# The float64 weight conversion of an attention and FFN kernel: the sign word made on GpSimd, the exponent offset in ScalarE's absolute value

## The chip, the cores and the metric

The kernel runs on one core of a Trainium2 chip. The metric is the device time of one execution in microseconds. The engines are named as in the profile: PE is TensorE's matmul and PEld its weight load, DVE is VectorE, ACT is ScalarE, POOL is GpSimd, SP the queue that issues the DMAs. Each engine takes its instructions in order; a wait on another engine is a semaphore.

## The reference

```
q, k, v: (8, 8, 576, 64) float32; tau = 0.02
scores = (q @ k^T) / 8
thresh = max(scores, -1) - tau
scores = where(scores >= thresh, scores, -1e9)
attn   = exp(scores - max(scores));  attn /= sum(attn) + 1e-9
x      = (attn @ v) as (4608, 512)
h      = maximum(x @ w_in, 0)          # w_in (512, 2048), float64
out    = (h * h) @ w_out               # w_out (2048, 512), float64
```

The two weight matrices are the only float64 inputs: a random float32-like array times a Python float stays double. No engine computes in float64, so the kernel makes float32 out of pairs of 32-bit words: the high word holds sign, 11 bits of exponent and 20 of the fraction, the low word the rest of the fraction.

## The kernel before, in words

The program has two large parts. In the first (some 500 us) the attention runs in **periods** `p`; in each, two units of 128 query rows by two heads go through a software pipeline: scores on PE, four row maxima ("top", line 452) on DVE, exponentials ("pow", 462) on ACT, four threshold masks with sums ("mask", 467) on DVE, transposes of the weights (fills U, V, W; line 380) on PE with evictions on ACT (523), and the product with v (532) on PE. Small steps in between: "leastA" and "leastB" (459) add tau to the maxima and "over" (474) adds 1e-9 to the sums of the period before, all on GpSimd; "inv" (477) is the reciprocal of what "over" made, on DVE. The second part computes the FFN with a fast matrix multiplication in seven products at two levels; the weights' sums are made on GpSimd in the periods behind the conversion.

The order of every engine's work in a period is written out by hand as a list of step names: `PLAIN` for ordinary periods and `CONVERTING` (597) for periods 2 to 34, in which weights are converted. A name of this list is looked up in `steps` (691) and issues its instructions, so the list is the program order of each engine's queue; all lines of one engine follow that order.

Conversion takes one chunk of 128 by 512 weights a period, 32 chunks in all. `fetch` loads the chunk two periods ahead into one of four buffers (`raw`), as pairs of words; `pick` gives its low words `lo` and its high words `hi`, each with a step of two words. The steps, as they are before:

- c1 (`convert1`, 205), ACT: `a` = absolute value of `hi` read as float32. As a float32 the high word has 8 bits of the double's exponent in its exponent field and the last 3 at the head of its fraction.
- c2 (`convert2`, 212), GpSimd: `lo` as unsigned times 2^-29, written back as an integer: the three top bits of the low word, rounded.
- c3 (`convert3`, 219), GpSimd: clamps `a` between two floats, so that the exponent fits float32.
- c4 (`convert4`, 227), DVE: `a` shifted left by 3 and cut by a mask, in place.
- c5 (`convert5`, 235), DVE: `hi` keeps its two top bits and takes the rest from `a`.
- c6 (`convert6`, 245), GpSimd: `hi` plus `lo`, as integers, gives the float32 weight; for the second half of the chunks it is stored to DRAM.

In a period the chunk begun in it goes through c1, c3 and c2, and the chunk begun in the period before through c4, c5 and c6. In conversion periods ACT copies the product with v out of PSUM (657) and GpSimd scales it by the reciprocals ("xm", 669). The order of GpSimd's instructions in a conversion period is c3, leastA, over, leastB, c2, c6, xm; that of DVE's is the four tops, c4, inv, maskA1, maskA0, maskB0, c5, maskB1. The second hunk of the diff that has DVE instructions, in the hidden layer (1195 to 1211), serves chunks that are left for later; with 16 of the 16 output chunks converted early there are none.

Of the kernel before, what the change touches and what calls it, by code (L numbers as in the profile page):

```python
# [10 lines left out]
FP32 = mybir.dt.float32  # L11
I32 = mybir.dt.int32
U32 = mybir.dt.uint32
ALU = mybir.AluOpType
AF = mybir.ActivationFunctionType
# [33 lines left out]
def kernel(  # L49
# [25 lines left out]
    nc = tc.nc  # L75
# [97 lines left out]
    raws, parts = {}, {}  # L173
# [23 lines left out]
    def pick(t, k):  # L197
        return t.rearrange("p (n two) -> p n two", two=2)[:, :, k]

    def convert1(m):  # L200
        if m not in raws:
            return
        lo, hi = pick(raws[m], 0), pick(raws[m], 1)
        a = cv.tile([P, WC], I32, tag="a", bufs=3, name="a")
        nc.scalar.activation(out=a.bitcast(FP32), in_=hi.bitcast(FP32), func=AF.Abs)
        parts[m] = (lo, hi, a)
        raws.pop(m)

    def convert2(m):
        if m in parts:  # L210
            lo = parts[m][0]
            nc.gpsimd.tensor_scalar(out=lo, in0=lo.bitcast(U32), scalar1=2.0**-29, scalar2=None, op0=ALU.mult)

    def convert3(m):
        if m not in parts:
            return
        a = parts[m][2].bitcast(FP32)
        low, high = (0x38000000, 0x47EFFFFF)
        nc.gpsimd.tensor_scalar(
            out=a, in0=a, scalar1=as_float(high), scalar2=as_float(low), op0=ALU.min, op1=ALU.max  # L220
        )

    def convert4(m):
        if m not in parts:
            return
        lo, hi, a = parts[m]
        nc.vector.tensor_scalar(
            out=a, in0=a, scalar1=3, scalar2=0x3FFFFFFF, op0=ALU.logical_shift_left, op1=ALU.bitwise_and
        )

    def convert5(m):
        if m not in parts:
            return
        lo, hi, a = parts[m]
        nc.vector.scalar_tensor_tensor(
            out=hi, in0=hi, scalar=-(1 << 30), in1=a, op0=ALU.bitwise_and, op1=ALU.bitwise_or
        )

    def convert6(m):
# [248 lines left out]
    for g in range(2, 2 * len(pairs)):  # L488
        two, x = divmod(g - 4, 4)
# [28 lines left out]
    def filled(m, f, pt, at=None):  # L518

        first, count = FILLS[f]  # L520
        count += 2 * (f == "W")
        to = wT[m][:, ds(weight_at(first) * P, count * P)]
        touch("weights", nc.scalar.copy(joined(to), whole(pt, 0, count)), at, 2 * BANK, m)  # L523
# [35 lines left out]
    def has(n):  # L559
        return 0 <= n < NU  # L560
# [22 lines left out]
    def converts(p):  # L583
        return is_wide and (has_chunk(p) or has_chunk(p - 1))
# [4 lines left out]
    def begun(n):  # L589
        return starts.get(n)  # L590
# [4 lines left out]
        maskB1  # L595
    """.split()
    CONVERTING = """
        fetch SA U eU T SB topA0 s1 c1 topA1 topB0 c3 V PV leastA over powA0 topB1
        powA1 powB0 c4 eT inv x maskA1 maskA0 W leastB maskB0 c5 eV c2 powB1 c6 eW maskB1 xm
    """.split()  # L600

    BEGIN_WITH = {
# [10 lines left out]
    def spots():  # L613
        return [(sc[:, ds(b * BANK + REST, (FULL + 1) * HALF)], b * BANK) for b in (1, 4)]

    def middle():
        return sc[:, 2 * BANK : 4 * BANK].rearrange("p (r n) -> p r n", r=2)

    def period(p):

        A, B_, a, b = 2 * p, 2 * p + 1, 2 * p - 2, 2 * p - 1
        m, turns = p - 2, TURNS.get(p, ())
        late, pt = {"W": []}, {}

        def fills(f, m):
            if has(2 * m):
                pt[f] = pt_pool.tile([P, 2, BANK], FP32, tag="pt", name="pt")
                fill(m, f, pt[f])

        def evict(f, m):  # L630
            if has(2 * m):
                filled(m, f, pt[f], 2 * BANK if f == "W" else None)

        def W():
            if has(2 * m + 2):
                pt["W"] = middle()
                fill(m + 1, "W", pt["W"], 2 * BANK)

        def turn_some():
            free = None  # L640
            if turns and p < 2:
                pq = pt_pool.tile([P, 2, BANK], FP32, tag="pt", name="pq")
                free = [(pq[:, r, :], None) for r in range(2)]
            late["turn"] = [turn(g // 2, g % 2, free or spots()) for g in turns]

        def PV():
            if has(2 * m):
                values(m)

        def values_out():  # L650
            if not has(2 * m):
                return
            late["x"] = x = sb.tile([P, 2, P], FP32, tag="x", bufs=2, name="x")
            for j in range(2):
                from_ = sc[:, ds(5 * j * BANK, P)]
                if converts(p):
                    made = nc.scalar.copy(x[:, j, :], from_)
                else:
                    made = nc.vector.tensor_tensor(  # L659
                        out=x[:, j, :], in0=from_, in1=wT[m][:, ts(SCALE_AT + j, P)], op=ALU.mult  # L660
                    )
                touch("x", made, 5 * j * BANK, P, m)

        def given_out():
            if has(2 * m):
                x = late.pop("x")
                if converts(p):
                    both = x[:, :, :].rearrange("p j n -> p (j n)")
                    nc.gpsimd.tensor_tensor(out=both, in0=both, in1=wT[m][:, ds(SCALE_AT * P, 2 * P)], op=ALU.mult)
                wT.pop(m)  # L670
                valued(m)
                give_x(m, x)
            ask(False)

        def scored_a():
            if has(A):
                scores(A, False)
                scores(A, True)
                scores(B_, True)
                softmax(A)  # L680

        def scored_b():
            if has(A):
                scores(B_, False)
                softmax(B_)

        def every(key):
            for then in late.get(key, ()):
                then()

        steps = {
            "U": lambda: fills("U", m), "V": lambda: fills("V", m + 1), "W": W, "T": turn_some,
            "eU": lambda: evict("U", m), "eV": lambda: evict("V", m + 1), "eW": lambda: evict("W", m + 1),
            "eT": lambda: every("turn"),
            "SA": scored_a, "SB": scored_b,
            "PV": PV, "x": values_out, "xm": given_out,
            "c1": lambda: convert1(begun(p)), "c2": lambda: convert2(begun(p)),
            "c3": lambda: convert3(begun(p)), "c4": lambda: convert4(begun(p - 1)),
            "c5": lambda: convert5(begun(p - 1)), "c6": lambda: convert6(begun(p - 1)),
            "s1": lambda: sums_due(p) and sums_step(), "s2": lambda: sums_due(p) and p < 60 and sums_step(), "fetch": lambda: fetch(begun(p + 2)),  # L700
        }
        steps["over"] = lambda: do(a, "over")
        steps["inv"] = lambda: do(a, "inverse")
        for letter, n in (("A", A), ("B", B_)):
            for what, name in (("least", "least"),):
                steps[what + letter] = lambda n=n, name=name: do(n, name)
            for what, name in (("top", "top"), ("pow", "power"), ("mask", "mask")):
                for j in range(2):
                    steps[f"{what}{letter}{j}"] = lambda n=n, name=name, j=j: do(n, name, j)
        for name in BEGIN_WITH.get(p) or (CONVERTING if converts(p) else PLAIN):  # L710
            steps[name]()
        for n in (A, B_):
            if has(n) and units[n][1] == FULL:
                for i in units[n][0]:
                    turned.pop(i)
# [403 lines left out]
    with tc.manual_schedule():  # L1119
# [54 lines left out]
        def convert_out(n, tick):  # L1174
# [3 lines left out]
            for j, (i, (m, k, h)) in enumerate(mine):  # L1178
# [3 lines left out]
                a = arena[:, ds(own[j], BANK // 2)]  # L1182
                key, step = ("out", i), tick - BEGIN - 2 * j
# [9 lines left out]
                lo, hi = pick(raw.bitcast(I32), 0), pick(raw.bitcast(I32), 1)  # L1193
                if step == 0:
                    b = b_pool.tile([P, BANK], FP32, tag="b", name="cw")[:, 0 : BANK // 2]
# [1 line left out]
                    parts[key] = (lo, hi, b.bitcast(I32))  # L1197
                    convert2(key)
                if step == 2:
                    low, high = (0x38000000, 0x47EFFFFF)  # L1200
                    b = parts[key][2].bitcast(FP32)
                    nc.vector.tensor_scalar(
                        out=b, in0=b, scalar1=as_float(high), scalar2=as_float(low), op0=ALU.min, op1=ALU.max
                    )
                    convert4(key)
                    convert5(key)
                if step == 5:
                    parts.pop(key)
                    nc.gpsimd.tensor_tensor(out=a.bitcast(I32), in0=hi, in1=lo, op=ALU.add)
# [99 lines left out]
def as_float(bits):  # L1309
    import struct  # L1310

    return struct.unpack("<f", struct.pack("<I", bits))[0]
# [30 lines left out]
```

## Time and profile before

| | |
|---|---|
| time, median of 3 runs | 1300.32 us (1298.04, 1300.32, 1300.54) |
| span of the profiled execution | 1298.2 us |
| busy share of the span | PE 98%, PEld 86%, DVE 78%, ACT 65%, POOL 71% |
| conversion periods | from 22.9 us (first maximum of period 2) to 257.2 us (first of period 35) |
| attention periods behind them | to about 500 us |

The span goes from the first to the last instruction on the slowest core; the times are those of separate executions, whose median lies 2.1 us above the span. In the timelines, a row is the start in us, the length in us, engine, line, operation, and the tiles written and read; in brackets stands how long the engine was idle before and what ended it. An engine's rows overlap by up to 0.1 us, so distances from start to start are used for sums. Line 452 and line 467 each consist of two instructions, the operation and a short read of its accumulator.

| row | engine | count | mean, ns |
|---|---|---|---|
| c1, line 205 | ACT | 32 | 699 |
| c2, line 212 | POOL | 32 | 2035 |
| c3, line 219 | POOL | 32 | 613 |
| c4, line 227 | DVE | 32 | 431 |
| c5, line 235 | DVE | 32 | 682 |
| c6, line 245 | POOL | 32 | 1478 |
| xm, line 669 | POOL | 33 | 725 |

### The profile page before, as it was taken

The page shows a single profiled execution, that of the slowest core. Times are in us where ns is not written, and L with a number is a line of the kernel's source. Part 1 is how long each engine was busy: PE and PEld are TensorE (multiplying, and loading weights), DVE is VectorE, ACT ScalarE, POOL GpSimd, SP SyncE. Part 2 cuts the span into 40 slices and gives each one's busy share as a digit, 9 for nine tenths or more (in the row PEclk, how much of TensorE's full clock was granted, in tenths as well). Part 3 has the DMA queues.
Part 4 walks back from the last instruction along what each step waited for, and adds up shares of the span by engine and source line. Part 5 has one row for each costly group of instructions (what it writes and reads, how often), then busy time and mean ns, then how long its engine had stood idle before and what let it go on. Part 6 is the DMA issues. An engine that isn't in the chain of part 4 may idle for free.

```text
span 1298.2 us, 45819 instructions
## 1 busy us (share of the span) xinstructions
PE 1276.4 (98%) x18287; PEld 1117.7 (86%) x18287; DVE 1007.0 (78%) x2423; ACT 845.5 (65%) x1498; POOL 926.8 (71%) x1031
## 2 busy tenths in 40 slices
PE   8999999999999999999999999999999999999998
PEld 5777777677777778988888888999999999999998
DVE  6999999999999996886887878867646654665463
ACT  6999999888998984666765856675523432343240
POOL 2787878755555321888897989858787767777775
PEclk8999999999999999999999999999999999999999
DMA  5665566544333312667768768589554224522411
GB/s 143 163 160 154 153 192 180 149 103 110 85 79 80 92 34 64 191 183 218 212 186 226 218 175 235 162 304 391 195 159 164 83 86 159 163 80 88 160 34 34
DMA packets 291413, 196.20 MB, mean 151 GB/s; under 512 B 100096, under 2 KB 252160, under 8 KB 291200
## 3 DMA queue, kind: packets, MB, share of 16 engines
q1 hardware_dynamic: 289888, 192.87, 51.5%
q8 instruction: 144, 2.36, 0.8%
q14 instruction: 69, 0.57, 0.2%
q10 hardware_dynamic: 1312, 0.41, 0.1%
HBM read 120.85 MB, written 72.35 MB: 149 GB/s over the span
## 4 chain that ended last, share of the span: by engine, by line
PE 86%; ACT 5%; DVE 4%; DMA 3%; issue 2%; POOL 0%; SPq 0%; ACTq 0%; DVEq 0%; POOLq 0%
PE po L1077 28%; PE ph L935 16%; PE sc L532 11%; PE sc L434 10%; PE ph L942 10%; PE pt L380 6%; DVE arena L452 2%; PE sc L515 2%; PE sc L398 2%; ACT arena L462 1%; ACT arena L523 1%; DMA g<-arena 1%; PE sc L380 1%; DVE arena L125 1%; DMA wall<-w 1%
## 5 line engine op out<-in xcount | busy, mean ns | idle before, releaser
L125 POOL TENSOR_TENSOR arena<-arena 128x512 f32<-128x512 f32 (+1 forms) x314 | 378.1, 1222 | 147.0 <-DVE arena L125 119.3
L1077 PE MATMUL po<-wall,arena 128*128 128x128 f32 x3528 | 395.0, 275 | 1.9 <-ACT arena L752 1.4
L1077 PEld LDWEIGHTS po<-wall,arena 128*128 128x128 f32 x3528 | 394.4, 192 | 2.5 <-ACT arena L752 1.8
L125 DVE TENSOR_TENSOR arena<-ph,arena 128x512 f32<-128x512 f32 x378 | 255.1, 689 | 79.9 <-PE ph L935 31.5
L122 POOL TENSOR_TENSOR arena<-arena 128x128 f32<-128x128 f32 (+1 forms) x322 | 265.4, 825 | 23.0 <-DMA arena<-w 6.6
L935 PE MATMUL ph<-arena,wall 128*128 128x256 f32 x1176 | 256.6, 380 | 1.8 <-DVE arena L125 1.4
L935 PEld LDWEIGHTS ph<-arena,wall 128*128 128x128 f32 x1176 | 222.2, 190 | 35.9 <-DVE arena L125 5.4
L125 DVE TENSOR_TENSOR arena<-po,arena 128x128 f32<-128x128 f32 x378 | 108.2, 290 | 167.7 <-PE po L1077 163.4
L467 DVE SCALAR_TENSOR_TENSOR arena<-arena 128x576 f32<-128x576 f32 x288 | 235.7, 855 | 0.9 <-ACT arena L462 0.9
L791 ACT COPY c<-arena 128x512 f32<-128x512 f32 (+1 forms) x295 | 169.0, 578 | 71.8 <-DVE arena L122 35.8
L452 DVE TENSOR_SCALAR_CACHE_REDUCE arena<-sc 128x576 f32<-128x576 f32 x288 | 205.1, 748 | 10.9 <-ACT arena L523 4.3
L462 ACT ACTIVATE arena<-arena 128x576 f32<-128x576 f32 x288 | 208.7, 773 | 7.4 <-DVE arena L452 4.2
L532 PEld LDWEIGHTS sc<-arena 64*64 64x64 f32 x5760 | 159.2, 133 | 36.5 <-DVE arena L452 19.8
L532 PE MATMUL sc<-arena 64*64 64x128 f32 (+1 forms) x5760 | 180.5, 262 | 2.9 <-DVE arena L452 1.3
L434 PE MATMUL sc<-arena 64*64 64x64 f32 (+1 forms) x2304 | 176.2, 415 | 3.8 <-ACT arena L403 2.4
L523 ACT COPY arena<-pt 128x1024 f32<-128x1024 f32 x144 | 146.4, 1016 | 27.9 <-PE pt L380 26.5
L122 DVE TENSOR_TENSOR arena<-arena,c 128x512 f32<-128x512 f32 x235 | 154.4, 666 | 11.0 <-ACT c L791 7.6
L752 ACT COPY arena<-po 128x128 f32<-128x128 f32 x63 | 16.6, 264 | 186.4 <-PE po L1077 183.7
L942 PE MATMUL ph<-arena,wall 128*128 128x128 f32 x1176 | 132.0, 275 | 0.7 <-DVE arena L659 0.7
L942 PEld LDWEIGHTS ph<-arena,wall 128*128 128x128 f32 x1176 | 131.6, 192 | 1.1 <-issue 0.8
L380 PEld LDWEIGHTS pt<-ident,arena 64*128 64x128 f32 x2304 | 83.5, 139 | 40.0 <-ACT arena L523 30.1
L434 PEld LDWEIGHTS sc<-arena 64*64 64x64 f32 x2304 | 74.0, 134 | 42.2 <-issue 14.1
(54 smaller groups left out, 1079.7 us busy)
## 6 DMA issues: line engine op xcount, KB each, us to landing
arena<-g SPq DMA_DIRECT2D x144, 256.0 KB, 4.4
g<-arena SPq DMA_DIRECT2D x192, 128.0 KB, 2.9
w<-arena SPq DMA_DIRECT2D x60, 256.0 KB, 2.8
wall<-w SPq DMA_DIRECT2D x49, 256.0 KB, 5.2
g<-arena SPq DMA_DIRECT2D x48, 256.0 KB, 3.8
arena<-w SPq DMA_DIRECT2D x44, 256.0 KB, 3.3
arena<-in_v_dram SPq DMA_DIRECT2D x32, 288.0 KB, 3.8
out_dram<-arena SPq DMA_DIRECT2D x70, 128.0 KB, 2.2
```

Source lines behind the costliest of these rows:

```text
L122: e.tensor_tensor(out=out, in0=x, in1=y, op=ALU.subtract)
L125: e.tensor_tensor(out=out, in0=x, in1=y, op=ALU.add)
L380: made = nc.tensor.transpose(pt[:, r, ts(slot, HALF)], of[rows, :], ident[rows, rows])
L434: made = nc.tensor.matmul(sc[at, ds(to, count)], lhs, kT[rows, ds(at_k, count)], start=True, stop=True)
L452: made = nc.vector.tensor_scalar(out=s[:, j, :], in0=sc[:, ds(at, S)], scalar1=1.0, scalar2=None, op0=ALU.mult, op1=ALU.min, accum_out=nmx ...
L462: nc.scalar.activation(out=w[:, :, j, :], in_=of(j), func=AF.Exp, bias=nmx[:, j : j + 1], scale=-1.0)
L467: nc.vector.scalar_tensor_tensor(out=w[:, :, j, :], in0=of(j), scalar=thr[:, j : j + 1], in1=w[:, :, j, :], op0=ALU.is_le, op1=ALU.mult, a ...
L532: made = nc.tensor.matmul(sc[ds(u * D, D), ds(5 * j * BANK + row, count)], loaded_v[i][rows, (c - (u != j)) % CH, :], wT[m][rows, ds(weigh ...
L791: nc.scalar.copy(c, y)
L935: nc.tensor.matmul(to[:, 2 * j : 2 * j + 2, :], W_IN[m, k][:, ts(2 * h + j, P)], part_x(steps, k, m), start=(not more and j == 0), stop=Tr ...
L942: nc.tensor.matmul(to[:, j, :], W_IN[m, k][:, ts(j, P)], x, start=(not more and j == 0), stop=True, skip_group_check=True,)
L1077: nc.tensor.matmul(to, g[:, j, :], w[:, j, :], start=(not more and j == 0), stop=(j == 3), skip_group_check=True)
```

## The change

ScalarE's absolute value takes a scale of 2^16, which adds 16 to the exponent field as it is read, so that after the shift by 3 nothing is left above the wanted bits and no mask is needed; c3's bounds move by the same 16. The new c4 runs on GpSimd: it makes out of `hi`, read as float32, a word that holds the sign alone (0 or -2^31), in place. c5, on VectorE, is then one instruction that shifts `a` and ORs it with this word. The old c4 on VectorE is gone. c4 now belongs to the chunk begun in the same period, like c1 to c3. In the list, GpSimd's c2 comes first in its part of the period, c4 follows c3, and c5 stands behind the first mask instead of the third: GpSimd's order is c2, c3, c4, leastA, over, leastB, c6, xm; DVE's is the four tops, inv, maskA1, c5, maskA0, maskB0, maskB1.

```diff
+    UP = 16
+    LOW, HIGH = (0x38000000, 0x47EFFFFF)
...
-        nc.scalar.activation(out=a.bitcast(FP32), in_=hi.bitcast(FP32), func=AF.Abs)
+        nc.scalar.activation(out=a.bitcast(FP32), in_=hi.bitcast(FP32), func=AF.Abs, scale=2.0**UP)
...
-        low, high = (0x38000000, 0x47EFFFFF)
+        low, high = (x + (UP << 23) for x in (LOW, HIGH))
...
     def convert4(m):
-        lo, hi, a = parts[m]
-        nc.vector.tensor_scalar(
-            out=a, in0=a, scalar1=3, scalar2=0x3FFFFFFF, op0=ALU.logical_shift_left, op1=ALU.bitwise_and
+        hi = parts[m][1]
+        nc.gpsimd.tensor_scalar(
+            out=hi, in0=hi.bitcast(FP32), scalar1=0.0, scalar2=-(2.0**31), op0=ALU.is_lt, op1=ALU.mult
         )
...
     def convert5(m):
         nc.vector.scalar_tensor_tensor(
-            out=hi, in0=hi, scalar=-(1 << 30), in1=a, op0=ALU.bitwise_and, op1=ALU.bitwise_or
+            out=hi, in0=a, scalar=3, in1=hi, op0=ALU.logical_shift_left, op1=ALU.bitwise_or
         )
...
     CONVERTING = """
-        fetch SA U eU T SB topA0 s1 c1 topA1 topB0 c3 V PV leastA over powA0 topB1
-        powA1 powB0 c4 eT inv x maskA1 maskA0 W leastB maskB0 c5 eV c2 powB1 c6 eW maskB1 xm
+        fetch SA U eU T SB topA0 s1 c1 c2 topA1 topB0 c3 c4 V PV leastA over powA0 topB1
+        powA1 powB0 eT inv x maskA1 c5 maskA0 W leastB maskB0 eV powB1 c6 eW maskB1 xm
     """.split()
...
-            "c3": lambda: convert3(begun(p)), "c4": lambda: convert4(begun(p - 1)),
+            "c3": lambda: convert3(begun(p)), "c4": lambda: convert4(begun(p)),
```

A last hunk, in the hidden layer's conversion of left-over chunks, writes the old c4 and c5 out in place, since it goes on using them.

More of the change, by code (lines that the diff above doesn't have):

```diff
@@ L1199, in convert_out @@
                 if step == 2:
-                    low, high = (0x38000000, 0x47EFFFFF)
-                    b = parts[key][2].bitcast(FP32)
+                    b = parts[key][2]
                     nc.vector.tensor_scalar(
-                        out=b, in0=b, scalar1=as_float(high), scalar2=as_float(low), op0=ALU.min, op1=ALU.max
-                    )
-                    convert4(key)
-                    convert5(key)
+                        out=b.bitcast(FP32), in0=b.bitcast(FP32), scalar1=as_float(HIGH), scalar2=as_float(LOW),
+                        op0=ALU.min, op1=ALU.max,
+                    )
+                    nc.vector.tensor_scalar(
+                        out=b, in0=b, scalar1=3, scalar2=0x3FFFFFFF, op0=ALU.logical_shift_left, op1=ALU.bitwise_and
+                    )
+                    nc.vector.scalar_tensor_tensor(
+                        out=hi, in0=hi, scalar=-(1 << 30), in1=b, op0=ALU.bitwise_and, op1=ALU.bitwise_or
+                    )
                 if step == 5:
```

## The prediction

> **What bounds the kernel now.** I first read the table of busy time by stretches, to see which stage the change meets and which engine is full there. The conversion steps run only from 22.9 to 257.2 us; the rows below are one stretch with them and one from the attention periods behind them (columns: PE, PEld, DVE, ACT, POOL busy, each with its count, then clock, DMA share, GB/s).
>
> ```profile
> 140.00:180.00 40.00, 39.31 (x946) 28.87 (x944) 40.00 (x107) 38.51 (x69) 31.82 (x38) 1.00 0.64 170
> 300.00:340.00 40.00, 40.00 (x1087) 30.30 (x1079) 38.96 (x117) 36.09 (x57) 23.54 (x32) 1.00 0.47 112
> ```
>
> With conversion VectorE has not one free moment in 40 us; without it TensorE has none. GpSimd looks idle for a fifth of the time. But an average hides order, so I took the timelines of VectorE and GpSimd over one period (start, length).
>
> ```profile
> 174.13 0.42 DVE L227 TENSOR_SCALAR arena<-arena 128x512 int32<-128x512 int32 x1
> 174.47 0.16 DVE L477 RECIPROCAL arena<-arena 128x4 f32<-128x4 f32 x1
> 174.55 0.78 DVE L467 SCALAR_TENSOR_TENSOR arena<-arena 128x576 f32<-128x576 f32 x1
> ...
> 175.27 1.22 DVE L467 SCALAR_TENSOR_TENSOR arena<-arena 128x576 f32<-128x576 f32 x1
> ...
> 176.42 0.81 DVE L467 SCALAR_TENSOR_TENSOR arena<-arena 128x576 f32<-128x576 f32 x1
> ...
> 177.16 0.68 DVE L235 SCALAR_TENSOR_TENSOR arena<-arena 128x512 int32<-128x512 int32 x1
> 177.77 0.81 DVE L467 SCALAR_TENSOR_TENSOR arena<-arena 128x576 f32<-128x576 f32 x1
> ...
> 178.50 0.75 DVE L452 TENSOR_SCALAR_CACHE_REDUCE arena<-sc 128x576 f32<-128x576 f32 x1
> ```
>
> ```profile
> 172.35 0.72 POOL L669 TENSOR_TENSOR arena<-arena 128x256 f32<-128x256 f32 x1
> 173.04 0.62 POOL L219 TENSOR_SCALAR arena<-arena 128x512 f32<-128x512 f32 x1
> 173.64 0.30 POOL L459 TENSOR_SCALAR arena<-arena,tau_p 128x2 f32<-128x2 f32 x1
> 174.00 0.23 POOL L474 TENSOR_SCALAR arena<-arena 128x4 f32<-128x4 f32 x1
> 174.32 0.38 POOL L459 TENSOR_SCALAR arena<-arena,tau_p 128x2 f32<-128x2 f32 x1
> 174.78 2.04 POOL L212 TENSOR_SCALAR arena<-arena 128x512 int32<-128x512 uint32 x1
> 177.99 1.48 POOL L245 TENSOR_TENSOR arena<-arena 128x512 int32<-128x512 int32 x1 [1.17 <-DVE arena L235]
> 179.44 0.72 POOL L669 TENSOR_TENSOR arena<-arena 128x256 f32<-128x256 f32 x1
> 180.13 0.61 POOL L219 TENSOR_SCALAR arena<-arena 128x512 f32<-128x512 f32 x1
> ```
>
> A period is 7.08 us (180.13 less 173.04 is 7.09). There are two rings. VectorE's own: its instructions follow each other without a gap. GpSimd's: c3, leastA and "over" (L474) must be done before the reciprocal (L477), which stands before the masks (L467); c5 (L235) stands behind three masks; c6 (L245) waits for c5; xm (L669) and the next c3 stand behind c6. By start-to-start distances: c3 0.60, leastA 0.36, "over" 0.23 and 0.04 to the reciprocal (210.01 to 210.05 where it waited), reciprocal 0.08, masks 0.72, 1.15 and 0.74, c5 0.61, hand-over 0.22, c6 1.45, xm 0.69: 6.89 us. So GpSimd, 76% busy in this stage, is 0.2 us short of setting the period: the reciprocal could have started at 174.27 and did at 174.47.
>
> One mask of the four lasts 1.22 instead of 0.81, and it is the one that begins while c2 (L212) runs. In the last conversion period, which has c4 and c5 but no c2, that mask is
>
> ```profile
> 254.40 0.81 DVE L467 SCALAR_TENSOR_TENSOR arena<-arena 128x576 f32<-128x576 f32 x1
> ```
>
> and the period lasts 6.68 us (250.54 to 257.22).
>
> **The change part by part.**
>
> *Abs with a scale, other bounds, c5 with shift and OR.* Same engine, shape and count: 32 ACTIVATEs of 0.70, 32 clamps of 0.61, 32 merges of 0.68 us. c5 keeps one plain and one strided input. I take 0; a tenth of the row either way is at most 0.07 us a period. The hunk in the weight conversion of the hidden layer adds nothing: its lines issue no instruction in this trace.
>
> *c4 leaves VectorE.* Minus 0.34 us a period (174.13 to 174.47). *c2 leaves the masks* for the start of GpSimd's part, beside the four row maxima (L452, which read PSUM): minus 0.41 (1.15 against 0.74). VectorE's ring falls from 7.08 to 6.33. The periods without conversion average 6.57 (the first plain "over" is at 263.73, the 36th behind it at 500.32), so that would be the next limit, TensorE being full there.
>
> *GpSimd's ring gets longer,* and this decides. c2 and the new c4 now stand between c3 and leastA's place: leastA and "over", which the reciprocal and with it all masks wait for, are queued behind c2, c3 and c4. c5 has come forward, behind the first mask only, which takes two masks out of the ring. Walked again: c2 2.04, c3 0.60, leastA 0.36, "over" 0.27, reciprocal 0.08, one mask 0.72, c5 0.61, hand-over 0.22, c6 1.45, xm 0.69: 7.04 us before c4. The 1.15 and 0.74 of two masks went out, c2's 2.04 came in. c2 can't begin earlier: it is behind xm on an in-order engine. The 1.17 us wait before c6 mostly vanishes: it was the only room that the ring had.
>
> *c4 on GpSimd* is not in the trace (float in, word out, both with a step of two words, two operations). From below the clamp c3, same engine, two operations, plain float: 0.61. From above c2, same steps and word output: 2.04, of which 0.49 is a wait for the mask in progress (174.78 to 175.27), so 1.55. It shares its input type and operation count with the one and steps and output with the other; I take the middle, 1.08, and keep 0.61 and 2.04.
>
> *Contention moves.* c2 beside the maxima saves its wait of 0.49, so 1.55; it could fall to about 0.83 if the 0.72 that the stretched mask then ran was also a stall of c2. Against that, c6 and xm now run beside the three masks left behind c5; before, only one mask followed c5. A leastB (L459) beside a mask shows the price: 0.90 us at 210.11 instead of leastA's 0.30. xm may lose 0.66 (the rest of a mask that c6 has pushed back), or nothing; I take 0.3.
>
> *Sum.* Ring 7.04 - 0.49 + 1.08 + 0.3 = 7.93 us, 0.85 more than 7.08. L212 is there 32 times, so 32 periods: 27 us. Nothing behind gives it back: the number of later periods and their order are fixed, and TensorE is full there. Span 1298.2 + 27 = 1325 us; the median shown is 2.1 above that span: 1327 us.
>
> The Trainium skill has a rule that would make c4 cheaper: by "GPSIMD Engine Reference", section 7, a read with steps of at most 8 bytes costs about 1.9 cycles an element, an estimate of 0.81 us for 512 at the page's 1.2 GHz; the sum would be 7.66 a period, some 1319 us. The rows do not bear it out for c2, which has the same step and takes 1.55 behind its wait, unless it was stalled in it.
>
> SP's queue is not passed by anything: fetch stays first, its buffer of four is freed by c6, still a period ahead of use. ACT's and TensorE's orders are unchanged; c1 ends before c3 needs it.
>
> **The rivals.**
>
> *Faster: c2's price is contention.* If c2 is stalled by the masks rather than slow, beside the maxima it costs 0.61 to 0.83, and c4 the same: ring 7.04 - 1.43 + 0.61 = 6.22 (6.66 by 0.83 for both), plus whatever xm and c6 lose. It decides as soon as the ring is under 7.08: c2 and c4 together under 2.08 us with no loss at c6 and xm, under 1.78 with my 0.3. At best the period is 6.57: 32 x 0.51 = 16 us, 1284; by 6.7, 1288. For it: c2 always ends about 0.40 us after the stretched mask. Against it: behind its wait c2 takes 1.54 to 1.62 in every period I read, and c6 and xm take c2's place beside the masks, so VectorE gives back some of its 0.41.
>
> The page "SBUF — State Buffer" of the Trainium skill, section "Who interferes with whom", says that a VectorE instruction with two SBUF inputs contends with a GpSimd instruction that reads SBUF; the 1.15 against 0.74 agrees, and by that rule alone the moved c2 is a gain.
>
> *Much slower: c4 like c2 in full.* 2.04 for c4, xm losing 0.66 and c2 still catching the last mask: 7.04 + 2.04 + 0.66 = 9.74, 85 us, 1385. With 1.55 for c4: 9.25, 69 us, 1370.
>
> *A wait in place of the one removed.* c2 writes the low words of a buffer whose high words c1 reads. If that is ordered as an overlap, c2 waits for c1, which in this trace ends 4.82 us behind the reciprocal (174.47 to 179.29): 4.82 + 1.55 + 0.60 + 1.08 + 0.36 + 0.27 = 8.68, 51 us, 1351. Before, c2 stood behind c3, which waits for c1 anyway, so the trace can't tell.
>
> *No effect.* Gain and loss cancel within 0.08 us a period: 1300.
>
> **How the numbers follow.** My forecast (1307 to 1345, c4 between 0.61 and 1.55) 0.60; the wait for c1 0.10; much slower 0.15; faster 0.11; no effect 0.04. About 0.2%, 2.6 us, is what a measurement of this kernel can tell from no change. Faster 0.11, same 0.04, slower 0.85. The range takes in the forecast, the wait and half of the much slower case: 1301 to 1372 us.
>
> **What would show it.** Right: in the changed profile VectorE waits before the reciprocal for GpSimd's "over" in every conversion period, GpSimd has no gap in them, and the period is 7.5 to 8.5 us; c4's row is 0.6 to 1.6 us; the masks beside c6 or xm are the stretched ones and none is beside c2. Wrong: VectorE still without a gap, c2 under 1 us, or c2 waiting for ACT (c1) at the period's start. If c4 is as cheap as the clamp and c2 halves, the sign is wrong.

## The result, and the profile after

| | before | after |
|---|---|---|
| time, median of 4 runs each | 1299.18 us | 1382.17 us |
| ratio | | 1.064 (95% interval 1.063 to 1.066) |
| span of the profiled execution | 1298.2 us | 1380.5 us |
| first maximum of period 2 to that of period 35 | 22.9 to 257.2 us | 21.4 to 339.6 us |
| one conversion period | 7.08 us | 9.78 us |

The kernel became 6.4% slower, 83 us. The conversion stage alone is 83.8 us longer (318.2 against 234.4 us) and starts 1.4 us earlier, which is the whole difference of the spans, 82.3 us. Everything behind it is only shifted. Of the executions behind the times below, one of `e4_c2_front` lasted 6592 us, which nothing on record explains; it is left out of that kernel's median.

The same stretch of the busy-time table (PE, PEld, DVE, ACT, POOL, then clock, DMA share, GB/s), now of the changed kernel:

```profile
140.00:180.00 40.00, 29.34 (x703) 20.06 (x700) 30.65 (x72) 28.81 (x53) 35.69 (x34) 1.00 0.43 111
```

VectorE, full before, is idle for a quarter of the time, and GpSimd has become the busiest engine. The waits say what VectorE waits for. These are VectorE's and GpSimd's timelines over one period of the changed kernel (the numbers of the lines have grown by 3: L470 masks, L238 c5, L480 reciprocal, L477 "over", L462 leastA and leastB, L215 c2, L222 c3, L230 the new c4, L248 c6, L672 xm):

```profile
170.62 0.18 DVE L480 RECIPROCAL arena<-arena 128x4 f32<-128x4 f32 x1 [2.12 <-POOL arena L477]
170.72 0.79 DVE L470 SCALAR_TENSOR_TENSOR arena<-arena 128x576 f32<-128x576 f32 x1
...
171.43 0.69 DVE L238 SCALAR_TENSOR_TENSOR arena<-arena 128x512 int32<-128x512 int32 x1
172.03 0.81 DVE L470 SCALAR_TENSOR_TENSOR arena<-arena 128x576 f32<-128x576 f32 x1
...
172.77 1.59 DVE L470 SCALAR_TENSOR_TENSOR arena<-arena 128x576 f32<-128x576 f32 x1
...
174.29 1.27 DVE L470 SCALAR_TENSOR_TENSOR arena<-arena 128x576 f32<-128x576 f32 x1
...
180.40 0.18 DVE L480 RECIPROCAL arena<-arena 128x4 f32<-128x4 f32 x1 [2.12 <-POOL arena L477]
180.50 0.79 DVE L470 SCALAR_TENSOR_TENSOR arena<-arena 128x576 f32<-128x576 f32 x1
...
181.21 0.69 DVE L238 SCALAR_TENSOR_TENSOR arena<-arena 128x512 int32<-128x512 int32 x1
```

```profile
172.27 1.48 POOL L248 TENSOR_TENSOR wall<-arena 128x512 int32<-128x512 int32 x1 [0.69 <-DVE arena L238]
173.71 1.24 POOL L672 TENSOR_TENSOR arena<-arena 128x256 f32<-128x256 f32 x1
175.03 1.98 POOL L215 TENSOR_SCALAR arena<-arena 128x512 int32<-128x512 uint32 x1
177.09 0.61 POOL L222 TENSOR_SCALAR arena<-arena 128x512 f32<-128x512 f32 x1
177.78 2.02 POOL L230 TENSOR_SCALAR arena<-arena 128x512 int32<-128x512 f32 x1
179.78 0.29 POOL L462 TENSOR_SCALAR arena<-arena,tau_p 128x2 f32<-128x2 f32 x1
180.14 0.23 POOL L477 TENSOR_SCALAR arena<-arena 128x4 f32<-128x4 f32 x1
180.46 0.90 POOL L462 TENSOR_SCALAR arena<-arena,tau_p 128x2 f32<-128x2 f32 x1
182.05 1.47 POOL L248 TENSOR_TENSOR wall<-arena 128x512 int32<-128x512 int32 x1 [0.69 <-DVE arena L238]
183.49 1.24 POOL L672 TENSOR_TENSOR arena<-arena 128x256 f32<-128x256 f32 x1
184.81 1.96 POOL L215 TENSOR_SCALAR arena<-arena 128x512 int32<-128x512 uint32 x1
```

In all conversion periods but the first two and the last, VectorE stands about 2.1 us in front of the reciprocal. The ring, the chain of steps that comes back to its own start once a period, can be read straight from the starts: c6 at 172.27 waited for c5; xm, c2, c3 and c4 follow with pauses of at most 0.09 us; leastA and "over" are queued behind them; the reciprocal starts when "over" is done (180.40); one mask and c5 later the next c6 starts, at 182.05. 182.05 less 172.27 is 9.78.

### The profile page after: what moved, and what is told of

It reads as the page before. It is cut to its first block, busy times and chain, and to the rows that moved or that the text cites. A ratio compares the mean times of both kernels' runs of the same rounds, so it can differ in the third digit from the quotient of the medians.

```text
span 1380.5 us, 45816 instructions
## 1 busy us (share of the span) xinstructions
PE 1290.2 (93%) x18287; PEld 1115.4 (81%) x18287; DVE 1025.9 (74%) x2391; ACT 847.9 (61%) x1498; POOL 1021.9 (74%) x1063
## 4 chain that ended last, share of the span: by engine, by line
PE 69%; issue 9%; POOL 8%; DVE 7%; ACT 6%; DMA 1%; SPq 0%; ACTq 0%; DVEq 0%; POOLq 0%
PE po L1080 28%; PE ph L938 16%; PE ph L945 10%; PE sc L535 5%; PE sc L437 5%; POOL arena L230 5%; DVE arena L470 5%; PE pt L383 3%; ACT arena L465 3%; POOL arena L222 1%; DVE arena L455 1%; ACT arena L526 1%; PE sc L401 1%; PE sc L518 1%; POOL arena L462 1%
## 5 line engine op out<-in xcount | busy, mean ns | idle before, releaser
L470 DVE SCALAR_TENSOR_TENSOR arena<-arena 128x576 f32<-128x576 f32 x288 | 263.6, 952 | 0.0
L535 PEld LDWEIGHTS sc<-arena 64*64 64x64 f32 x5760 | 165.8, 138 | 48.7 <-DVE arena L455 35.2
L535 PE MATMUL sc<-arena 64*64 64x128 f32 (+1 forms) x5760 | 189.2, 269 | 10.8 <-DVE arena L455 9.8
L437 PE MATMUL sc<-arena 64*64 64x64 f32 (+1 forms) x2304 | 172.6, 413 | 2.9 <-ACT arena L406 2.3
L383 PE MATMUL pt<-ident,arena 64*128 64x64 f32 x2304 | 109.0, 230 | 34.6 <-DVE arena L470 30.8
```

Source lines behind the costliest of these rows:

```text
L383: made = nc.tensor.transpose(pt[:, r, ts(slot, HALF)], of[rows, :], ident[rows, rows])
L437: made = nc.tensor.matmul(sc[at, ds(to, count)], lhs, kT[rows, ds(at_k, count)], start=True, stop=True)
L470: nc.vector.scalar_tensor_tensor(out=w[:, :, j, :], in0=of(j), scalar=thr[:, j : j + 1], in1=w[:, :, j, :], op0=ALU.is_le, op1=ALU.mult, a ...
L535: made = nc.tensor.matmul(sc[ds(u * D, D), ds(5 * j * BANK + row, count)], loaded_v[i][rows, (c - (u != j)) % CH, :], wT[m][rows, ds(weigh ...
```

## The experiments

Theory A is the one on record: the ring through GpSimd's queue and the reciprocal sets the period. Rivals: B, GpSimd simply has too much work, in whatever order; C, the masks stretched by contention make the loss. A second question was why the new c4 takes 2.03 us. All times stand beside runs of the kernel before on the same chip (medians 1296.9 to 1298.0 us), and a loss is counted from these; the changed kernel's is 83 us. In the texts on record 1299 or 1300 was used.

**c4 left out** (`e1_no_c4`): the sign's instruction is not issued.

```diff
-        nc.gpsimd.tensor_scalar(
-            out=hi, in0=hi.bitcast(FP32), scalar1=0.0, scalar2=-(2.0**31), op0=ALU.is_lt, op1=ALU.mult
-        )
+        return
```

> The changed kernel without GpSimd's c4: the sign word is left out, the high word is ORed in as it is. Theory A, the ring (xm, c2, c3, c4, leastA, over, reciprocal, one mask, c5, c6): it is 9.78 us in the changed kernel, so 9.78 - 2.08 = 7.7 us here and the kernel stays slower than before, some 1319 us. Theory B, GpSimd is simply overloaded, whatever the order: its work falls from 8.75 to 6.7 us a period, under the 7.08 of before, so 1285 to 1300 us. Theory C, contention with the masks: the masks beside c6 and xm stay stretched (1.59 and 1.27 us), VectorE sums to about 7.6, 1316 us, with VectorE never waiting for over.

Measured: 1317.28 us, ratio 1.015 (1.014 to 1.017), period 7.68 us. B falls: GpSimd's load, some 6.6 us a period (103.62 of the 120 us from 100 to 220), is under the 7.08 of before, and the kernel is still slower. A and C gave nearly the same number here. The trace shows why (here L475 is "over" and L478 the reciprocal):

```profile
145.94 0.23 POOL L475 TENSOR_SCALAR arena<-arena 128x4 f32<-128x4 f32 x1
146.20 0.18 DVE L478 RECIPROCAL arena<-arena 128x4 f32<-128x4 f32 x1
```

The reciprocal starts 0.03 us behind "over" (146.20 against 145.94 plus 0.23), but VectorE is also busy for 119.67 of these 120 us, with the masks of 1.59 and 1.28 us. The two limits meet, so this run doesn't tell A from C.

**c5 put back behind the third mask** (`e8_c5_late`) tells them apart.

```diff
-        powA1 powB0 eT inv x maskA1 c5 maskA0 W leastB maskB0 eV powB1 c6 eW maskB1 xm
+        powA1 powB0 eT inv x maskA1 maskA0 W leastB maskB0 c5 eV powB1 c6 eW maskB1 xm
```

> The changed kernel with c5 put back behind the third mask, all else as changed. Theory A: two masks of 0.74 us come into the ring, xm loses its 0.52 and c2 up to 0.46 of waiting: 10.3 to 10.8 us a period, 1400 to 1417 us. Theory C: c6 and xm meet one mask instead of three, the masks are no longer stretched by 1.24 us a period, so it is faster than the changed kernel, about 1345 us.

Measured: 1399.30 us, ratio 1.078 (1.076 to 1.080), period 10.36 us: the ring's arithmetic. The loss is 102 us against 83 of the changed kernel, though no mask is stretched any more (all 0.79 to 0.82 us), as in these two:

```profile
149.76 0.81 DVE L470 SCALAR_TENSOR_TENSOR arena<-arena 128x576 f32<-128x576 f32 x1
...
151.10 0.81 DVE L470 SCALAR_TENSOR_TENSOR arena<-arena 128x576 f32<-128x576 f32 x1
```

C as the cause falls. GpSimd's rows of this kernel also give prices without a mask beside them:

```profile
152.77 0.73 POOL L672 TENSOR_TENSOR arena<-arena 128x256 f32<-128x256 f32 x1
153.58 1.63 POOL L215 TENSOR_SCALAR arena<-arena 128x512 int32<-128x512 uint32 x1
155.30 0.61 POOL L222 TENSOR_SCALAR arena<-arena 128x512 f32<-128x512 f32 x1
155.97 2.00 POOL L230 TENSOR_SCALAR arena<-arena 128x512 int32<-128x512 f32 x1
```

xm falls from 1.24 to 0.73 and c2 from 1.98 to 1.63; c4 stays at 2.00, so c4's price owes nothing to contention.

**The small steps first** (`e3_small_first`): leastA, over and leastB ahead of c2, c3 and c4.

```diff
-        fetch SA U eU T SB topA0 s1 c1 c2 topA1 topB0 c3 c4 V PV leastA over powA0 topB1
-        powA1 powB0 eT inv x maskA1 c5 maskA0 W leastB maskB0 eV powB1 c6 eW maskB1 xm
+        fetch SA U eU T SB topA0 s1 c1 topA1 topB0 V PV leastA over powA0 topB1
+        powA1 powB0 eT inv x maskA1 c5 maskA0 W leastB c2 c3 c4 maskB0 eV powB1 c6 eW maskB1 xm
```

> The changed kernel with leastA, over and leastB ahead of c2, c3 and c4 in GpSimd's queue; all instructions the same. Theory A: the reciprocal no longer waits behind c2 to c4, the ring is broken and GpSimd's own load of 8.0 to 8.8 us a period sets the time: 1329 to 1354 us, GpSimd without a gap. Theory B: the load is the same, so the period stays near 9.8 us less the 0.7 us gap before c6: about 1360 us or more. Theory C: c2 and c4 now run beside masks as well and stretch them further: not under 1382 us.

Measured: 1349.54 us, ratio 1.040 (1.039 to 1.042), period 8.64 us, in A's window. The loss is 53 us instead of 83: 30 us come back by order alone. GpSimd runs through from c6 to c6 without waiting for another engine: its load is now the limit, with c4 at 2.45 and c3 at 0.81 us beside masks.

**The order of before, with the new c4 behind c2** (`e5_old_order`), c5 behind the third mask.

```diff
-        fetch SA U eU T SB topA0 s1 c1 c2 topA1 topB0 c3 c4 V PV leastA over powA0 topB1
-        powA1 powB0 eT inv x maskA1 c5 maskA0 W leastB maskB0 eV powB1 c6 eW maskB1 xm
+        fetch SA U eU T SB topA0 s1 c1 topA1 topB0 c3 V PV leastA over powA0 topB1
+        powA1 powB0 eT inv x maskA1 maskA0 W leastB c2 c4 maskB0 c5 eV powB1 c6 eW maskB1 xm
```

> The changed kernel's instructions in the order of before: c3, leastA, over, leastB, c2, then the new c4, c6, xm on GpSimd, c5 behind the third mask. Theory A: over no longer stands behind c2 and c4; c4 is longer than the 1.17 us that GpSimd had free, so its own chain sets the period: 0.60 + 0.36 + 0.32 + 0.46 + 2.05 + 2.03 to 2.44 + 1.04 to 1.45 + 0.70 = 7.6 to 8.4 us, 1315 to 1342 us, most of the loss gone by order alone. Theory C: only VectorE's sum counts, 7.08 - 0.34 + 0.42 for one more stretched mask = 7.16, 1302 us.

Measured: 1333.87 us, ratio 1.028 (1.026 to 1.029), period 8.28 us. So of the loss of 83 us some 36 (1333.9 less 1297.7) come with the new instructions in the old order, and the other 47 with the new order. GpSimd is the limit here too: c6 follows c4 at once, where it waited 1.17 us for c5 before.

```profile
150.71 2.11 POOL L230 TENSOR_SCALAR arena<-arena 128x512 int32<-128x512 f32 x1
152.77 1.05 POOL L248 TENSOR_TENSOR wall<-arena 128x512 int32<-128x512 int32 x1
```

**c2 alone moved to the front** (`e4_c2_front`), in the kernel before.

```diff
-        fetch SA U eU T SB topA0 s1 c1 topA1 topB0 c3 V PV leastA over powA0 topB1
-        powA1 powB0 c4 eT inv x maskA1 maskA0 W leastB maskB0 c5 eV c2 powB1 c6 eW maskB1 xm
+        fetch SA U eU T SB topA0 s1 c1 c2 topA1 topB0 c3 V PV leastA over powA0 topB1
+        powA1 powB0 c4 eT inv x maskA1 maskA0 W leastB maskB0 c5 eV powB1 c6 eW maskB1 xm
```

> The kernel before, with c2 alone moved to the start of GpSimd's part; c4 and c5 stay on VectorE as they were. Theory A, the ring: c2 2.06 joins c3 0.60, leastA 0.36, over 0.27, reciprocal 0.08, three masks of 0.72 to 0.74, c5 0.61, hand-over 0.22, c6 1.45, xm 0.69: 8.5 us against 7.08, some 1345 us. Theory C, contention: no mask runs beside c2, VectorE needs 6.67 us a period, 1286 us.

Measured: 1335.87 us, ratio 1.029 (1.027 to 1.031), period 8.36 us against A's 8.5: c2 costs 1.61 to 1.66 here instead of 2.06, while xm takes 0.1 us more to the next start. The masks are all at 0.8 us, as C had it, and it loses all the same: VectorE waits some 1.06 us for "over" in nearly every conversion period.

```profile
147.55 1.61 POOL L212 TENSOR_SCALAR arena<-arena 128x512 int32<-128x512 uint32 x1
148.52 0.93 DVE L227 TENSOR_SCALAR arena<-arena 128x512 int32<-128x512 int32 x1
150.51 0.18 DVE L477 RECIPROCAL arena<-arena 128x4 f32<-128x4 f32 x1 [1.07 <-POOL arena L474]
```

**c4 with a float output and one operation** (`e2_float_sign`).

```diff
-            out=hi, in0=hi.bitcast(FP32), scalar1=0.0, scalar2=-(2.0**31), op0=ALU.is_lt, op1=ALU.mult
+            out=hi.bitcast(FP32), in0=hi.bitcast(FP32), scalar1=0.0, scalar2=None, op0=ALU.mult
```

> The changed kernel, with c4 as one multiplication of the high word (as float) by 0.0, written as a float: a zero that keeps the sign, the same bits as the word. If the output as an integer makes c4 dear, it falls from 2.03 to about 0.65 us, the ring to 8.4 us, the time to some 1341 us. If the step of two words makes it dear, it stays at 1.9 to 2.0 us and the time at 1378 to 1382 us.

Measured: c4 1.60 us, 1364.60 us, ratio 1.052 (1.050 to 1.053), period 9.23 us. Neither guess on the price holds. The ring accounts for the period: from start to start c4 takes 1.57 us instead of 2.00, and c3 0.58 instead of 0.69 (9.78 - 0.43 - 0.11 = 9.24).

**Eight forms of c4, then eight more** (`e6_forms`, `e7_forms2`), chosen by the chunk's number; `f` is the high word as a float, with a step of two words, `af` is `a`, plain. `two` stands for c4's own two operations; in `none` the second factor is 0.0. Two of the sixteen forms:

```diff
+        if m % 8 == 0:
+            nc.gpsimd.tensor_scalar(out=hi, in0=f, **two)
+        if m % 8 == 5:
+            nc.gpsimd.tensor_scalar(out=af, in0=af, **none)
...
```

> The changed kernel with c4 in eight forms, by the chunk's number, so that each has its own row; the weights come out different. Forms: float or word output, plain or with a step of two, plain or stepped input, one operation or two. If the integer output is the price, every form with word output takes about 2.0 us and every form with float output 0.6 to 0.7. If the step of the output is the price, the forms that write with a step take 2.0 whatever the type; if that of the input, those that read with a step.

Rows of the first set: as changed (236), float output (238), plain float throughout (246), one multiplication with steps (250); columns as in the groups of the page.

```profile
L236 POOL TENSOR_SCALAR arena<-arena 128x512 int32<-128x512 f32 x4 | 8.2, 2045 | 0.3
L238 POOL TENSOR_SCALAR arena<-arena 128x512 f32<-128x512 f32 x4 | 8.2, 2042 | 0.0
...
L246 POOL TENSOR_SCALAR arena<-arena 128x512 f32<-128x512 f32 x4 | 7.7, 1931 | 0.3
L250 POOL TENSOR_SCALAR arena<-arena 128x512 f32<-128x512 f32 x4 | 6.5, 1615 | 0.0
```

Neither the type nor the step is the price: a comparison and a multiplication take 1.93 us on plain floats and 2.05 in c4's form. The type costs nothing that shows here (2.045 against 2.042 us), the steps about 0.1 us.

> The changed kernel with c4 in eight further forms by the chunk's number; the weights come out without their signs' treatment. If the kind of operation makes the price, every form of min and max alone takes 0.6 to 0.7 us, with a step or a word output too, and every form with a multiplication or a comparison 1.6 (one operation) to 2.0 us (two). If min and max are cheap only in plain float form, the stepped and word forms of them take 1.9 to 2.0 us too.

Rows of the second set: max and mult, plain (245); is_lt alone (241), min alone (237) and mult alone (235), plain; min and max with steps, float (239) and word (247) output; mult and add, plain (249); min and max, plain, word output (243).

```profile
L245 POOL TENSOR_SCALAR arena<-arena 128x512 f32<-128x512 f32 x4 | 7.7, 1929 | 0.3
L241 POOL TENSOR_SCALAR arena<-arena 128x512 f32<-128x512 f32 x4 | 6.0, 1493 | 0.3
L237 POOL TENSOR_SCALAR arena<-arena 128x512 f32<-128x512 f32 x4 | 6.0, 1490 | 0.3
L235 POOL TENSOR_SCALAR arena<-arena 128x512 f32<-128x512 f32 x4 | 6.0, 1490 | 0.3
L239 POOL TENSOR_SCALAR arena<-arena 128x512 f32<-128x512 f32 x4 | 2.8, 708 | 0.0
L247 POOL TENSOR_SCALAR arena<-arena 128x512 int32<-128x512 f32 x4 | 2.8, 697 | 0.0
L249 POOL TENSOR_SCALAR arena<-arena 128x512 f32<-128x512 f32 x4 | 2.5, 623 | 0.3
L243 POOL TENSOR_SCALAR arena<-arena 128x512 int32<-128x512 f32 x4 | 2.5, 613 | 0.3
```

The expectation was half right. The pair of operations makes the price, but not by "min and max are cheap": a min alone takes 1.49 us, more than twice a min and a max together; mult with add is cheap, mult alone or behind max or is_lt is not. Why the pairs differ is not shown.

**A cheap c4, in the new order and in the old** (`e9_clamp_sign`, `e10_clamp_old_order`).

```diff
-            out=hi, in0=hi.bitcast(FP32), scalar1=0.0, scalar2=-(2.0**31), op0=ALU.is_lt, op1=ALU.mult
+            out=hi.bitcast(FP32), in0=hi.bitcast(FP32), scalar1=0.0, scalar2=-0.0, op0=ALU.min, op1=ALU.max
```

> The changed kernel with c4 as min with 0.0 and max with -0.0 on the high word as a float: a zero with the sign. In the forms a pair of min and max took 0.70 us with steps, so theory A has the ring at 9.78 - 2.03 + 0.70 = 8.45 us and the time at 1340 to 1345 us: with c4 cheap, the order alone still loses over 40 us. If c4's price were the whole loss, the time would be near 1298 us or below.

Measured: c4 0.70 us, 1337.13 us, ratio 1.030 (1.029 to 1.032), period 8.33 us. With c4 at a third of its price the new order still loses 39 of the 83 us.

> The same cheap c4, in the order of before, behind c2. GpSimd's chain is then 6.9 to 7.3 us a period. By theory A with the stretching of masks, VectorE saves 0.34 by c4 but one more mask is stretched by 0.42: 2.72 + 0.09 + 0.72 + 0.74 + 1.16 + 0.60 + 1.15 = 7.18 us against 7.08, so 1298 to 1305 us, no gain. If moving work off the full engine is a gain by itself, VectorE needs 6.74 us a period and the time is 1287 to 1290 us.

Measured: 1305.20 us, ratio 1.0059 (1.0047 to 1.0072), period 7.33 us: the best of the forms that were run, and still 0.6% slower than before. The old place of c2 has its stretched mask again, and c4 behind it stretches another, as this stretch of VectorE's timeline shows.

```profile
142.62 1.29 DVE L470 SCALAR_TENSOR_TENSOR arena<-arena 128x576 f32<-128x576 f32 x1
143.84 0.68 DVE L238 SCALAR_TENSOR_TENSOR arena<-arena 128x512 int32<-128x512 int32 x1
144.44 1.22 DVE L470 SCALAR_TENSOR_TENSOR arena<-arena 128x576 f32<-128x576 f32 x1
```

The 0.34 us that c4's removal gave VectorE is paid back by about 0.4 of stretching, and GpSimd's chain from c3 to c3 is 7.33 us without a wait for another engine. The two limits nearly meet again: VectorE is busy for 119.27 of 120 us, and the reciprocal starts 0.03 us behind "over". None of the versions that were run beat the kernel before.

One combination was not run: the cheap c4 with the small steps first. An estimate from the rows of `e3_small_first` is 6.9 us a period for GpSimd there (8.64 less c4's 2.39 plus 0.67) and 7.2 us for VectorE (8.64 less its wait of 1.46), against 7.08 before. No gain is to be expected from that, but none is excluded, since a shorter c4 might stretch fewer masks.

## Why the prediction was wrong

The mechanism on record was right: the ring, its members and their order, with VectorE waiting for "over" in all periods but three. The sign was right. The size was not: 1327 us was forecast, the range ended at 1372, and 1382 came. Two terms of the sum failed: the price of c4, and what the masks do to c2 and xm. The term by term account of one period (start to start, c2 at 175.03 to the next c2 at 184.81):

| term | forecast, us | measured, us |
|---|---|---|
| c4 | 1.08 | 2.00 |
| c2 | 2.04 - 0.49 | 2.06 |
| xm, with what masks cost it and c6 | 0.69 + 0.3 | 1.32 |
| c3 | 0.60 | 0.69 |
| all others (leastA, over, reciprocal, mask, c5, hand-over, c6) | 3.71 | 3.71 |
| sum | 7.93 | 9.78 |

- **The largest step that failed is c4's price.** "I take the middle, 1.08": it measured 2.00, and the 0.92 us between the two are half of the missing 1.85. With 2.00 in its place and all else as forecast, the sum is 8.85 us a period, some 1357 us, still inside the range. The rows were compared by data type and by step, and both are beside the point. On plain floats the same pair of operations costs 1.93 us; c3, the cheap row, is a pair of min and max, which stays at 0.61 us with a word output and 0.70 with steps. No row of before had another pair on wide tiles, so its trace could not show this; what it could show is that c2, one operation only, costs more than c3's two. I kept 2.04 as an end, and that end was the answer. The rule that the prediction cites from the Trainium skill ("GPSIMD Engine Reference", section 7; an estimate of 0.81 us for a read with steps of 8 bytes) is not borne out either: min and max with such steps take 0.70 us, is_lt and mult without any step 1.93.
- **c2's saving of 0.49 did not come**: its term is 0.51 above the forecast. c2 does last 1.60 to 1.66 us away from masks, as `e8_c5_late` and `e4_c2_front` show, with a pause of some 0.08 behind it. But in the changed kernel the last mask is pushed back beside xm, and c2 starts while that mask runs: at 175.03 with the mask until 175.49. I had this as "c2 still catching the last mask" in the much slower rival, not in the forecast.
- **xm's loss was 0.63, not 0.3.** Of it 0.51 is the mask's (xm lasts 1.24 us, and 0.73 in `e8_c5_late` with no mask beside it), somewhat less than the 0.66 that I had priced as the rest of a pushed-back mask. The other 0.12 is a pause before c2, which stands in `e8_c5_late` too: c2 starts there 0.81 us behind xm's start. c3's 0.09 is of that kind as well (0.67 there). The order of the rows reads as one chain: c6 pushes back maskB0 (1.59 us), that delays xm; xm pushes back maskB1 (1.27 us), that delays c2. I took half of the first and none of the second where the walk, done to its end, gives both.
- **The rival "much slower" was the case that came**: 9.74 us a period and 1385 us on record, 9.78 and 1382.17 measured. It had 0.15; the range took in only its lower part.
- **The other rivals.** "Faster" needed c2 and c4 together under 1.8 to 2.1 us; they take 4.06. Its mechanism, that c2 is mostly stalled, is partly true: 0.4 of 2.0 us. The wait of c2 for c1 did not appear: in the changed kernel c2 follows xm by 0.08 us, but c1 had ended 0.31 us before c2 began (174.72 against 175.03), so this trace can't tell whether c2 would wait for it. "VectorE's ring falls to 6.33" is not what the order gives: where "over" is nearly in time, in `e1_no_c4`, VectorE needs 7.6 us, since c6 and xm stretch masks by 0.78 and 0.46 us. The change would have lost there too.
- **Signs and readings.** The waits for "over" and the stretched masks beside c6 and xm came as written. "GpSimd has no gap" did not: 0.69 us stay before c6, and the ring on record, with a mask, c5 and the hand-over between the reciprocal and c6, leaves room for one. Nor did "none is beside c2". GpSimd was 80% busy in the stage before (31.82 of 40 us), not the 76% in the text on record; the ring doesn't rest on it.

The page "SBUF — State Buffer" of the Trainium skill, section "Who interferes with whom", names the pairing that the rows show: VectorE's masks, with two inputs in SBUF, against GpSimd's reads. The trace agrees with it in both directions, 0.81 to 1.59 us for a mask beside c6 and 0.73 to 1.24 us for xm beside a mask.

## What to carry to other kernels

When work leaves a full engine for an engine with idle time, follow the receiving engine's queue: what stands behind the new work, and who waits for that. Here a step of 0.23 us, queued behind 4.75 us of conversion, held up the engine that was to be relieved. Price an instruction that the trace does not have by its arithmetic operations first, and where the ends are a factor of three apart, measure it or let the forecast carry the dear end. Walk the new order to the end of the period: what is pushed back pushes back the next.

## What the runs showed of the hardware that was not expected

- On GpSimd a TENSOR_SCALAR over 128 by 512 takes 0.61 to 0.71 us with min and max or with mult and add, 1.49 us with mult, min or is_lt alone, and 1.93 us with max and mult or with is_lt and mult, all on plain floats or, for min and max, also with steps and a word output. With add behind mult, or max behind min, it took less than half the time of mult or min alone.
- A mask beside c6 is pushed back by 0.78 us, beside c2 or c4 by 0.4 to 0.5, although without a mask c2 (1.6 us) and c4 (2.0 us) last longer than c6 (1.04 us in `e5_old_order`).
- VectorE's old c4, 0.42 us, took 0.93 to 0.97 us when it began beside c2 (`e4_c2_front`), so a VectorE instruction with a single input in SBUF can be held up too.
- TensorE's granted clock between 100 and 220 us was 0.84 in `e8_c5_late`, 0.96 in `e2_float_sign` and 0.97 in the changed kernel, against 1.00 before and in the other runs with a time above. These three have the fewest matmuls in that stretch (2018 to 2226, the others 2372 or more); what lowers the clock is not shown. The rings above don't pass through TensorE.
